# Norms from the solved blocks, block copies on three engines, and separate PSUM tiles in the opening of a DeltaNet and maxout kernel

## The chip, the cores and the metric

The kernel runs on one NeuronCore of a Trainium2 chip. Five engines work side by side, each through its own list of instructions in order: TensorE (PE in the profile, with PEld for its weight loads), VectorE (DVE), ScalarE (ACT), GpSimd (POOL) and SyncE (SP, which here only issues DMAs). They meet at semaphores. The metric is the device time of one execution in microseconds (us); four runs of the kernel before gave 524.16, 525.88, 523.24 and 526.01 us, a median of 525.02 us.

## The reference

Two stages follow one another. The first is a delta-rule recurrence over 768 steps, for 4 batches and 8 heads of width 48; the second is a feed-forward layer with three hidden projections whose maximum is taken:

```python
k_n = k / (np.linalg.norm(k, axis=-1, keepdims=True) + 1e-06)
for t in range(S):
    y[:, :, t] = np.einsum('bhd,bhde->bhe', q[:, :, t], state)
    v_old = np.einsum('bhde,bhd->bhe', state, kt)
    state = state + bt[:, :, :, None] * np.einsum('bhd,bhe->bhde', kt, vt - v_old)
x = y.transpose(0, 2, 1, 3).reshape(B * S, H * D)        # 3072 x 384
h = np.maximum(np.maximum(x @ w1, x @ w2), x @ w3)       # 3072 x 768
out = h @ w_out
```

## The kernel before, in words

The 768 steps are cut into 12 chunks of 64 steps, and two chunks make a group (six groups). Inside a chunk the recurrence becomes matrix work: `gram` (L434 to L460) forms the products of keys with keys (`at`) and of keys with queries (`pt`); a triangular system of the keys' products, scaled with beta, is solved; its solution `ut` is applied to the values (`new`, tile `p_u`), and the result `u` gives the outputs (`to_y`, `p_y`) and updates the state (`step`, `p_s`). The feed-forward layer of group m, `ffn(m)`, then works on the 512 tokens of its two chunks (`p_h`, `p_o`).

The kernel uses k without its norm: the rows of the solved system are scaled by the norm's square, and the values of a chunk are multiplied with the norms (`scale`, L286, on GpSimd). For groups 1 to 5 the norms are read off the diagonal of the keys' products inside `solve` (`norms_of`, L273). Group 0 does this differently: ScalarE squares the four first key tiles (`first_squares`, L312), VectorE sums them (L318), TensorE swaps the halves of the odd ones (`flipped`, L327), ScalarE copies the swapped sums (L1024) and `first_norms` takes root and a Newton step (L261 to L266).

The order on every engine is the order in which the program is written (`manual_schedule`), so the opening, L1006 to L1084, is an order by hand. Its steps, as the profile names them:

- Keys of the first two chunks are loaded (`kpad`), turned on TensorE (`turn`, `p_t`, copied out at L367), and multiplied (`keys`, `p_g`, copied out as `at` at L455).
- `to_blocks` (L497, L499) copies the 32 x 32 blocks on the diagonal into one tile, one copy for each of four partition blocks of a unit n, 16 copies in all. `first_blocks` (L503) transposes that tile on VectorE.
- `solve(0)` takes the norms from the diagonal (L539 on), scales, and eliminates in 15 steps of two VectorE instructions (L565, L569) inside 16 x 16 blocks. The result is transposed back (L573) and copied into `ut` for chunk 0, and later for chunk 1 (L584 on ScalarE, L586 on VectorE for chunk 0 and on GpSimd for chunk 1).
- The links of chunk 0 join the blocks: `halves_z` (`p_e`), `halves_u` (`p_f`), `join_z` (`p_z`), `join_u` (`p_j`). Then come `new` (`p_u`), `to_y` (`p_y`) and `to_x` (`p_x`, copied out as `xt` at L876 and L877), and with `xt` the first `p_h` of `ffn(0)`. For chunk 0 each link works on heads 0 to 3 and 4 to 7 in turn, each half in a PSUM tile of its own (`heads_of`); inside a half the two partition halves (`bb` 0 and 1) are copied out by ScalarE and VectorE, both from that one tile. PSUM tiles of this kind (`ps_two`) rotate through three buffers.
- Chunk 1's first link (`halves_z(1)`, again `p_e`) stands on TensorE between `to_y(0)` and `to_x(0)`. It reads `ut` of chunk 1.
- On GpSimd the order is: scale the values of chunk 0, scale the values of chunk 1 (loaded by `load_v(1)`, L139), two copies of `ut` for chunk 1 (L586), and then the sums that finish the converted weights (`w_sb`, L254).
- The weights arrive as 32-bit pieces that ScalarE takes apart in three instructions (`weights`, L238 to L240); VectorE shifts one part (L250) and GpSimd joins them. `some(conv, 1)` runs one such piece.

During `ffn(0)` the system of group 1 is solved on VectorE, with steps of 31 columns, between the steps of the feed-forward layer; from there on TensorE carries the kernel.

Of the kernel before, what the change touches and what calls it, by code (L numbers as in the profile page):

```python
# [9 lines left out]
FP32 = mybir.dt.float32  # L10
# [13 lines left out]
def kernel(  # L24
# [273 lines left out]
    nrm_0 = const.tile([128, 2, 2, H], FP32, name="nrm_0")  # L298

    ksum_0, kflip_0 = small("ksum0", 2, 2, H), small("kflip0", 2, H)  # L300

    def first_squares(units=range(4)):
        ksum, kflip, squares = ksum_0, kflip_0, []
        for n in units:
            c, g = divmod(n, 2)
            if n < 2:
                ksq = work.tile([128, H, D], FP32, name="ksq", tag="o_sb")
            else:
                ksq = in_wo(1).rearrange("p s r -> p (s r)")[
                    :, (n - 2) * H * D : (n - 1) * H * D  # L310
                ].rearrange("p (h d) -> p h d", h=H)
            nc.scalar.square(ksq, kpad[n][:, :, 0:D])  # L312
            squares.append(ksq)
        yield
        for n in units:
            c, g = divmod(n, 2)
            ksq = squares[n]
            nc.vector.tensor_reduce(  # L318
                out=kflip[:, c] if g else ksum[:, c, 0], in_=ksq,
                axis=mybir.AxisListType.X, op=ALU.add,  # L320
            )

    def flipped(kflip):
        p_n = ps_ffn([128, TOK], "p_n")[:, 0 : 2 * H]
        for bb in range(2):
            half = rows(1 - bb)
            nc.tensor.matmul(  # L327
                p_n[rows(bb)], ident[half, half],
                kflip[half].rearrange("p c h -> p (c h)"),
            )  # L330
        return p_n

    def first_norms():
        norm(nrm_0, ksum_0, small("root0", 2, 2, H), small("newton0", 2, 2, H))

# [185 lines left out]
    def solve(m):  # L521
# [15 lines left out]
        if m:  # L537
            norms_of(m, bl)
        nc.vector.reciprocal(bl, bl)  # L539
        nc.vector.tensor_tensor(out=bl, in0=bl, in1=bl, op=ALU.mult)  # L540
# [30 lines left out]
        if m == 0:  # L571
            back = in_rows(xs[0])
            nc.vector.transpose(out=back, in_=y.rearrange("p c i -> p i c"))  # L573
            yield
            for cc in range(2):
                for i in range(4):
                    bb, half = divmod(i, 2)
                    r = block(bb, half)
                    to = ut[cc][r, :, :, BL * half : BL * (half + 1)].rearrange(
                        "p g h i -> p (g h) i"  # L580
                    )
                    of = back[r, :, 16 * cc : 16 * (cc + 1)].rearrange("p i x -> p x i")
                    if half:
                        nc.scalar.copy(to, of)  # L584
                    else:
                        (nc.gpsimd if cc else nc.vector).tensor_copy(to, of)  # L586
                yield
            return
# [61 lines left out]
    def heads_of(c, name, w):  # L650
# [4 lines left out]
        for i, copy in enumerate(copies):  # L655
# [4 lines left out]
            )  # L660

    def span(hs):
        return slice(hs[0], hs[-1] + 1)
# [14 lines left out]

    def negated(bb, to, of, c=0):
        if bb and c < 1:  # L680
            nc.vector.tensor_scalar_mul(to, of, -1.0)
        else:
            nc.scalar.mul(to, of, -1.0)

    def halves_u(c):
        t, z = fine.pop(c), zs[c % NU]
        for hs, p_v, _ in heads_of(c, "p_f", BL):
            for i, h in enumerate(hs):
                for bb, g in TILES:
                    r = rows(bb ^ g)  # L690
                    nc.tensor.matmul(p_v[rows(bb), g, i], t[g][r, h], z[r, g, h])
            for f in (0, 1):
                for bb in range(2):
                    r = block(bb, f, HB)
                    negated(
                        bb,
                        ut[c % NU][r, :, span(hs), BL * f + HB : BL * (f + 1)],
                        p_v[r, :, :, HB * f : HB * (f + 1)],
                        c,
                    )  # L700

    def join_z(c):
        at = [ats.pop(2 * c + g) for g in range(2)]
        z, second = zs[c % NU], ut[c % NU][:, :, :, BL:C]
        for hs, p_v, _ in heads_of(c, "p_z", BL):
            for i, h in enumerate(hs):
                for bb, g in TILES:
# [3 lines left out]
                    )  # L711
            nc.scalar.copy(z[block(0), :, span(hs)], p_v[block(0)])
            copy = nc.vector.tensor_copy if c < 1 else nc.scalar.copy
            copy(z[block(1), :, span(hs)], p_v[block(1)])

    def join_u(c):
        z, t = zs[c % NU], t1[c % NU]
        u12 = ut[c % NU][:, :, :, BL:C]
        for hs, p_v, _ in heads_of(c, "p_j", BL):
            for i, h in enumerate(hs):  # L720
                for bb, g in TILES:
                    r = block(bb ^ g)
                    nc.tensor.matmul(p_v[block(bb), g, i], t[r, g, h], z[r, g, h])  # L723
            for bb in range(2):
                negated(bb, u12[block(bb), :, span(hs)], p_v[block(bb)], c)

# [89 lines left out]
    def to_x(c):  # L816
        m, cc = divmod(c, 2)
        if m not in xts:
            xts[m] = work.tile([128, KT, TOK], FP32, name="xt")
        y_f = yts.pop(c).rearrange("p g h d -> p g (h d)")  # L820
        p_x = ps_two("p_x")
        for g in range(2):
            for t in range(KT):
                nc.tensor.transpose(
                    p_x[:, g, t * 128 : (t + 1) * 128],
                    y_f[:, g, t::KT],
                    ident,
                )
        xt = xts[m][:, :, cc * 256 : (cc + 1) * 256].rearrange(
            "p t (g x) -> p g t x", g=2  # L830
        )
        copied(c, xt, p_x[:, :, 0 : KT * 128].rearrange("p g (t x) -> p g t x", t=KT))

# [26 lines left out]
    def turn_y(c):  # L860
# [8 lines left out]
        )  # L869

    def copied(c, to, of):

        if c:
            nc.scalar.copy(to, of)
        else:
            nc.scalar.copy(to[:, 0], of[:, 0])  # L876
            nc.vector.tensor_copy(to[:, 1], of[:, 1])  # L877


# [126 lines left out]
    turn(1, (0,), nc.vector.tensor_copy)  # L1006
    sums_0 = first_squares()
    some(sums_0, 1)
    keys(0, None, nc.vector.tensor_copy)
    some(sums_0, 1)  # L1010
    keys(1, None)
    to_blocks(0, (nc.gpsimd,) * 4)
    turn(2, (0,))
    turn(3, (0,))
    to_blocks(1, (nc.gpsimd,) * 4)
    keys(2, None, nc.vector.tensor_copy)
    keys(3, None, nc.vector.tensor_copy)
    to_blocks(2, (nc.scalar, nc.gpsimd, nc.scalar, nc.gpsimd))
    to_blocks(3, (nc.vector, nc.scalar, nc.vector, nc.scalar))
    first_blocks()  # L1020
    load_q(2, (nc.gpsimd, nc.gpsimd))
    some(solving, 1)
    p_n = flipped(kflip_0)
    nc.scalar.copy(ksum_0[:, :, 1], p_n.rearrange("p (c h) -> p c h", c=2))  # L1024
    turn(4, (0,))
    turn(5, (0,))
    keys(4)
    keys(5)
# [16 lines left out]
    gram(2, (1,), None, later=True)  # L1045
    turn(3, (1,))
    some(solving, HB + 1)
    halves_t(0)
# [3 lines left out]
    for c in range(2):  # L1052
        scale(c, nrm_0[:, c])
    some(conv, 1)
    halves_u(0)
# [176 lines left out]
```

## Time and profile before

| what | value |
|---|---|
| median of four runs | 525.02 us |
| profiled execution: time | 523.99 us |
| profiled execution: span | 522.3 us |
| TensorE busy | 495.5 us, 95% of the span |
| VectorE busy | 311.6 us, 60% |
| ScalarE busy | 164.2 us, 31% |
| GpSimd busy | 190.5 us, 36% |
| first `p_h` of `ffn(0)` starts | 51.63 us into the span |

The span is what lies between the first and the last recorded instruction of the profiled execution; its time is 1.7 us longer. A timeline line reads: start, duration, engine, line of the kernel, operation, tile written and tile read, shapes, count, and in brackets the idle time before with what ended it. A line of the stretches reads: stretch, its length, then for each engine its busy time and (in brackets) its instructions, then the granted TensorE clock (1.00 is full speed), the busy share of the DMA engines and GB/s.

### The profile page before, as it was taken

To read this page: it belongs to the slowest core of one execution; us is meant where nothing else is said; L and a number is where in the kernel's file an instruction comes from. 1 tells how busy PE (TensorE), PEld (TensorE's weight loads), DVE (VectorE), ACT (ScalarE), POOL (GpSimd) and SP (SyncE) were. 2 spreads that over 40 slices of the span, in tenths; PEclk is the share of its full clock that TensorE was granted. 3 is DMA by queue.
4 is the path that set the end of the run, shared out by engine and by line. 5 is a ranking of instruction groups with operands and counts; after the bars stand their busy time and mean duration, and the time that the engine had idled before them with its cause. 6 is when DMAs were issued, how large, how long until landed. Compare 5 with 4: busy or idle time off the path is not lost.

```text
span 522.3 us, 18030 instructions
## 1 busy us (share of the span) xinstructions
PE 495.5 (95%) x7840; PEld 306.9 (59%) x7840; DVE 311.6 (60%) x695; ACT 164.2 (31%) x302; POOL 190.5 (36%) x314
## 2 busy tenths in 40 slices
PE   7667998989999999999999999999999999999996
PEld 6556777855566655665555565655655555654453
DVE  6875999997996451699652988645896221111100
ACT  5557473777413142210153201252101411011000
POOL 7514255584474753951395770503130000000000
PEclk9865699999999999999999999999999999999999
DMA  8973968466026953454585453833333202220011
GB/s 110 208 164 106 162 161 145 128 147 200 15 72 151 177 102 67 128 133 116 110 155 127 116 133 92 166 48 92 82 105 86 43 3 63 62 60 0 0 30 32
DMA packets 108671, 53.47 MB, mean 102 GB/s; under 512 B 91760, under 2 KB 102928, under 8 KB 108592
## 3 DMA queue, kind: packets, MB, share of 16 engines
q1 hardware_dynamic: 97840, 34.44, 32.0%
q0 software_dynamic: 8640, 17.49, 13.5%
q8 instruction: 62, 1.02, 0.8%
q10 hardware_dynamic: 2112, 0.39, 0.5%
q14 instruction: 17, 0.14, 0.1%
HBM read 39.17 MB, written 13.11 MB: 100 GB/s over the span
## 4 chain that ended last, share of the span: by engine, by line
PE 77%; DVE 13%; ACT 3%; DMA 2%; issue 2%; SPq 1%; POOL 1%; DVEq 0%; ACTq 0%; POOLq 0%
PE p_h L926 33%; PE p_o L958 26%; DVE tmp L565 3%; PE p_g L438 3%; PE p_u L768 3%; DVE wo_sb L569 3%; PE p_m L906 2%; PE p_y L810 2%; DMA kmore<-in_k_dram 2%; PE p_k L740 2%; PE p_j L723 2%; PE p_s L791 1%; PE p_q L740 1%; SPq L120 1%; PE p_z L709 1%
## 5 line engine op out<-in xcount | busy, mean ns | idle before, releaser
L926 PE MATMUL p_h<-xt,w_sb 128*128 128x512 f32 (+1 forms) x522 | 219.0, 564 | 2.7 <-DVE h L940 1.3
L926 PEld LDWEIGHTS p_h<-xt,w_sb 128*128 128x128 f32 x522 | 96.1, 193 | 88.1 <-issue 79.9
L958 PE MATMUL p_o<-wo_sb,h 128*128 128x384 f32 x288 | 97.8, 489 | 0.0
L940 DVE TENSOR_TENSOR h<-h,p_h 128x512 f32<-128x512 f32 (+1 forms) x48 | 29.6, 617 | 89.7 <-PE p_h L926 89.5
L958 PEld LDWEIGHTS p_o<-wo_sb,h 128*128 128x128 f32 x288 | 53.7, 190 | 35.7 <-issue 0.5
L565 DVE TENSOR_TENSOR tmp<-x_bl,y_bl 128x31 f32<-128x31 f32 (+20 forms) x139 | 51.7, 372 | 4.1
L964 ACT COPY o_sb<-p_o 128x384 f32<-128x384 f32 x24 | 11.5, 479 | 132.9 <-PE p_o L958 126.8
L569 DVE TENSOR_TENSOR y_bl<-y_bl,tmp 128x31 f32<-128x31 f32 (+20 forms) x139 | 48.5, 349 | 4.8
L936 ACT ACTIVATE h<-p_h 128x512 f32<-128x512 f32 x30 | 17.9, 597 | 87.9 <-PE p_h L926 84.9
L958 PE MATMUL p_o<-w_sb,xt 128*128 128x384 f32 x120 | 42.0, 486 | 0.0
L396 POOL DMA_DIRECT2D turned<-in_q_dram x72 | 39.1, 551 | 3.5 <-POOL turned L391 3.0
L438 PE MATMUL p_g<-kqt 48*64 48x64 f32 (+1 forms) x1216 | 27.1, 236 | 6.4 <-DVE nt_bl L263 3.8
L438 PEld LDWEIGHTS p_g<-kqt 48*64 48x64 f32 x1216 | 24.0, 137 | 14.4 <-ACT kqt L367 7.4
L958 PEld LDWEIGHTS p_o<-w_sb,xt 128*128 128x128 f32 x120 | 22.8, 190 | 15.9
L287 POOL TENSOR_TENSOR v_t<-v_t,nrm 128x768 f32<-128x768 f32 x12 | 18.2, 1518 | 25.5 <-DVE nrm L266 12.4
L254 POOL TENSOR_TENSOR w_sb<-mant,up 128x384 int32<-128x384 int32 x18 | 18.3, 1018 | 24.8 <-DVE mant L250 19.1
L120 POOL DMA_DIRECT2D kpad<-in_k_dram x32 | 21.8, 689 | 14.6 <-PE p_s L791 13.2
L798 DVE TENSOR_TENSOR st<-st,p_s 48x768 f32<-48x768 f32 (+1 forms) x18 | 17.1, 949 | 15.0 <-PE p_s L791 14.8
L422 DVE TENSOR_TENSOR pt<-p_g,mask 128x512 f32<-128x512 f32 x20 | 13.7, 688 | 15.8 <-PE p_g L438 15.8
L139 POOL DMA_DIRECT2D v_t<-in_v_dram x12 | 9.9, 828 | 35.2 <-PE p_u L768 35.2
L391 POOL MEMSET turned<- 128x96 f32 x18 | 3.3, 191 | 44.0 <-DVE kqt L412 44.0
L768 PEld LDWEIGHTS p_u<-v_t,ut 64*64 64x64 f32 x768 | 13.5, 141 | 8.6 <-issue 7.4
(153 smaller groups left out, 628.1 us busy)
## 6 DMA issues: line engine op xcount, KB each, us to landing
w_bits<-in_moe_w_dram SPq DMA_DIRECT2D x14, 384.0 KB
out_dram<-o_sb SPq DMA_DIRECT2D x48, 96.0 KB
turned<-in_q_dram POOLq DMA_DIRECT2D x72, 48.0 KB, 2.5
kpad<-in_k_dram POOLq DMA_DIRECT2D x32, 96.0 KB, 5.4
y_x<-y SPq DMA_DIRECT2D x16, 192.0 KB
qall<-y_x SPq DMA_DIRECT2D x32, 96.0 KB
ut<-y_d SPq DMA_DIRECT2D x40, 64.0 KB
v_t<-in_v_dram SPq DMA_DIRECT2D x12, 192.0 KB
```

Source lines behind the costliest of these rows:

```text
L120: queues[bb].dma_start(out=dst[rows(bb ^ g), :, 0:D], in_=src[2 * bb + g, :, c * C : (c + 1) * C, :].rearrange("h p d -> p h d"),)
L254: nc.gpsimd.tensor_tensor(out=dst.bitcast(I32), in0=mant_v.bitcast(I32), in1=up_v, op=ALU.add)
L287: nc.gpsimd.tensor_tensor(out=vts[c], in0=vts[c], in1=nrm[:, :, :, None].to_broadcast([128, 2, H, D]), op=ALU.mult,)
L396: (queue, nc.gpsimd)[i].dma_start(out=t[p0 : p0 + 32, bb, at : at + NP * 2 * D].rearrange("p (j x) -> p j x", j=NP), in_=(k, q)[i][2 * bb ...
L438: nc.tensor.matmul(p_g[rows(bb ^ (g * i)), par, c0 : c0 + C * (1 + whole)], kq[:, 0], kq if whole else kq[:, i],)
L565: nc.vector.tensor_tensor(out=t_v, in0=row.to_broadcast(t_v.shape), in1=column.to_broadcast(t_v.shape), op=ALU.mult,)
L569: nc.vector.tensor_tensor(out=rest, in0=rest, in1=t_v, op=ALU.subtract)
L768: nc.tensor.matmul(p_v[rows(bb ^ g), g, i], ut[c % NU][rows(bb), g, h], rhs[rows(bb), g, h],)
L926: nc.tensor.matmul(p_h, w_sb[i][:, t, f * 128 : (f + 1) * 128], xt[:, t, lo : lo + w], start=(t == 0), stop=(t == KT - 1),)
L936: nc.scalar.activation(out=h, in_=p_h, func=mybir.ActivationFunctionType.Relu)
L940: nc.vector.tensor_tensor(out=h, in0=h, in1=p_h, op=ALU.max)
L958: nc.tensor.matmul(p_o, stays, moves, start=(n == 0), stop=(n == len(terms) - 1))
```

## The change

Five things are changed, all in the opening:

1. Norms of group 0. The squares, their sums, the swap on TensorE, the copy of the swapped sums, and the root with its Newton step are gone. `solve(0)` keeps its norms `bl` (the reciprocal goes to a tile of its own), and `first_norms` is one 128 x 32 transpose on VectorE.
2. Block copies. The 16 copies of `to_blocks` stood on GpSimd (10), ScalarE (4) and VectorE (2); now they stand on GpSimd (7), ScalarE (4) and VectorE (5). The first keys are turned and multiplied in another order and with other engines for the copies out.
3. Fourth block of chunk 0's `ut`: of the four copies of solved blocks VectorE takes three and ScalarE one (two and two before).
4. Evictions of `p_f` and `p_j` for chunk 0: the first four heads go to ScalarE alone; for the last four, each partition half has a PSUM tile of its own, one for ScalarE and one for VectorE. `p_z` of chunk 0 is copied out by ScalarE alone. `p_x` of chunk 0 stands in two tiles, one for each engine.
5. Order: `turn(4)` and `turn(5)` stand ahead of the first step of `solving`, and the first piece of weights is taken apart ahead of the elimination steps and not after the norms.

The core of the diff:

```diff
-    def first_squares(units=range(4)):
...
-            nc.scalar.square(ksq, kpad[n][:, :, 0:D])
...
-            nc.vector.tensor_reduce(
...
-    def flipped(kflip):
...
     def first_norms():
-        norm(nrm_0, ksum_0, small("root0", 2, 2, H), small("newton0", 2, 2, H))
+        nc.vector.transpose(out=nrm_0.rearrange("p c g h -> p (c g h)"), in_=bl_0[0])
...
         if m:
             norms_of(m, bl)
-        nc.vector.reciprocal(bl, bl)
+            nc.vector.reciprocal(bl, bl)
+        else:
+            bl_0.append(bl)
+            bl = small("inv_bl", BL)
+            nc.vector.reciprocal(bl, bl_0[0])
...
-                    if half:
+                    if i == 1 or cc and half:
                         nc.scalar.copy(to, of)
                     else:
                         (nc.gpsimd if cc else nc.vector).tensor_copy(to, of)
...
+    def negated_of(c, name, w):
+        if c:
+            p_v = ps_two(name)[:, :, 0 : H * w].rearrange("p g (h x) -> p g h x", x=w)
+            yield range(H), (p_v, p_v), (nc.scalar.mul,) * 2
+            return
+        p = [
+            ps_two(name)[:, :, 0 : NP * w].rearrange("p g (h x) -> p g h x", x=w)
+            for _ in range(3)
+        ]
+        yield range(NP), (p[0], p[0]), (nc.scalar.mul,) * 2
+        yield range(NP, H), (p[1], p[2]), (nc.scalar.mul, nc.vector.tensor_scalar_mul)
...
-            nc.scalar.copy(z[block(0), :, span(hs)], p_v[block(0)])
-            copy = nc.vector.tensor_copy if c < 1 else nc.scalar.copy
-            copy(z[block(1), :, span(hs)], p_v[block(1)])
+            for bb in range(2):
+                nc.scalar.copy(z[block(bb), :, span(hs)], p_v[block(bb)])
...
         p_x = ps_two("p_x")
         for g in range(2):
+            if g and not c:
+                p_x = ps_two("p_x")
...
+            if not c:
+                (nc.vector.tensor_copy if g else nc.scalar.copy)(xt[:, g], of[:, g])
+        if c:
+            nc.scalar.copy(xt, of)
...
-    sums_0 = first_squares()
-    some(sums_0, 1)
-    keys(0, None, nc.vector.tensor_copy)
-    some(sums_0, 1)
-    keys(1, None)
-    to_blocks(0, (nc.gpsimd,) * 4)
+    A, V, P = nc.scalar, nc.vector, nc.gpsimd
+    keys(0, None)
+    to_blocks(0, (P, P, P, P))
     turn(2, (0,))
+    keys(1, None, nc.vector.tensor_copy)
+    to_blocks(1, (V, P, V, P))
     turn(3, (0,))
-    to_blocks(1, (nc.gpsimd,) * 4)
-    keys(2, None, nc.vector.tensor_copy)
+    keys(2, None)
+    to_blocks(2, (A, P, A, A))
     keys(3, None, nc.vector.tensor_copy)
-    to_blocks(2, (nc.scalar, nc.gpsimd, nc.scalar, nc.gpsimd))
-    to_blocks(3, (nc.vector, nc.scalar, nc.vector, nc.scalar))
+    to_blocks(3, (V, A, V, V))
     first_blocks()
     load_q(2, (nc.gpsimd, nc.gpsimd))
-    some(solving, 1)
-    p_n = flipped(kflip_0)
-    nc.scalar.copy(ksum_0[:, :, 1], p_n.rearrange("p (c h) -> p c h", c=2))
     turn(4, (0,))
     turn(5, (0,))
+    some(solving, 1)
...
     turn(3, (1,))
+    some(conv, 1)
     some(solving, HB + 1)
...
-    some(conv, 1)
     halves_u(0)
```

## The prediction

> **What bounds the kernel now.** I read the stretches first, to see which engine carries which part of the span.
>
> ```profile
> 0.00:52.00 52.00, 34.75 (x903) 30.10 (x904) 36.02 (x86) 31.05 (x62) 23.90 (x48) 0.76 0.78 147
> 52.00:80.00 28.00, 26.44 (x638) 21.34 (x637) 26.74 (x63) 17.44 (x36) 11.75 (x13) 0.84 0.78 159
> 80.00:118.00 38.00, 34.48 (x689) 26.21 (x689) 35.71 (x72) 22.93 (x44) 24.57 (x33) 1.00 0.67 143
> 118.00:500.00 382.00, 381.90 (x5561) 218.95 (x5558) 213.11 (x477) 90.84 (x159) 130.28 (x223) 1.00 0.40 92
> ```
>
> TensorE (second column) is full from 118 us on. Of its 26.8 us without work, 17.25 lie in the first 52 us; from 52 to 118 VectorE is busy 62.45 of 66 us and the chain of waits runs through it almost alone. So a gain in the opening reaches the end by bringing the first `p_h`, and with it VectorE's dense stretch, forward.
>
> Next, the timelines of the opening, engine by engine. ScalarE and VectorE at the links of chunk 0:
>
> ```profile
> 34.80 0.54 ACT L238 ACTIVATE mant<-w_bits 128x384 f32<-128x384 f32 x1
> 36.21 0.24 ACT L683 ACTIVATE ut<-p_f 16x128 f32<-16x128 f32 x1
> 38.05 0.30 DVE L681 TENSOR_SCALAR ut<-p_f 16x128 f32<-16x128 f32 x1 [0.33 <-ACT ut L683]
> 39.77 0.76 DVE L714 COPY z<-p_z 32x256 f32<-32x256 f32 x2
> 41.35 0.85 DVE L681 TENSOR_SCALAR ut<-p_j 32x256 f32<-32x256 f32 x2
> 42.23 1.59 DVE L422 TENSOR_TENSOR pt<-pt,mask 128x512 f32<-128x512 f32 x1
> 50.93 0.56 DVE L877 COPY xt<-p_x 128x384 f32<-128x384 f32 x1 [3.30 <-ACT xt L876]
> ```
>
> The evictions of `p_f` start late (ScalarE takes weights apart until 36.33) and then take turns, each waiting for the other engine. Then GpSimd, and the queue that feeds it:
>
> ```profile
> 36.25 1.47 POOL L287 TENSOR_TENSOR v_t<-v_t,nrm 128x768 f32<-128x768 f32 x1 [12.41 <-DVE nrm L266]
> 41.80 1.47 POOL L287 TENSOR_TENSOR v_t<-v_t,nrm 128x768 f32<-128x768 f32 x1 [4.08 <-DMA v_t<-in_v_dram]
> 43.22 2.67 POOL L586 COPY ut<-x_bl 32x512 f32<-32x512 f32 x2
> ...
> 21.00 10.85 SPq L468 DMA_DIRECT2D at_d<-at  x16
> 34.50 1.34 SPq L139 DMA_DIRECT2D v_t<-in_v_dram  x2
> ```
>
> GpSimd's second scaling waits 4.08 us for the values of chunk 1, and the copies of chunk 1's `ut` are queued behind it until 45.89. Last, TensorE:
>
> ```profile
> 43.45 1.52 PE L768 MATMUL p_u<-v_t,ut 64*64 64x48 f32 x45 [0.95 <-issue]
> 44.70 2.04 PE L810 MATMUL p_y<-u,pt 64*64 64x48 f32 x64
> 46.52 2.38 PE L674 MATMUL p_e<-ut,at 64*64 64x32 f32 x64
> 48.84 1.55 PE L824 MATMUL p_x<-ident,y 128*128 128x128 f32 x6
> 51.63 2.90 PE L926 MATMUL p_h<-xt,w_sb 128*128 128x256 f32 x6 [1.25 <-DVE xt L877]
> ```
>
> The `p_e` at 46.52 is chunk 1's; it reads what GpSimd finished at 45.89, 0.6 us earlier: nearly a tie.
>
> **The change, part by part.** Times are of the profiled execution.
>
> *Head, to the transpose of the blocks at 13.03.* VectorE loses four sums (1.92 us, 8.23 to 10.15) and gains three copies (3 x 0.466 = 1.40); ScalarE loses four squares (2.5 us, with a wait of 0.61 for keys); GpSimd loses three of ten copies (1.29). Replayed in the new order with the rows' durations: the first product is copied out by ScalarE at 7.6 to 8.2, GpSimd's first four copies follow to 9.95 and its other three to 11.2; the last product is full at 10.7, VectorE copies it out (0.65) to 11.4, and then come VectorE's three copies to 12.5 or 12.9 and, after three for the product before, ScalarE's last to 12.3. So the transpose starts 0.1 to 0.5 us earlier, 0.3 taken. Worse is possible: were VectorE's five copies and GpSimd's seven to shut each other out, 5 x 0.466 + 7 x 0.431 = 5.35 us from 8.2 would give 13.55, 0.5 later. The rows speak against it: GpSimd's ten copies took 387 to 398 ns each, those beside VectorE's two (429 and 502 ns) too.
> [...]
>
> *`turn(4)`, `turn(5)` ahead of the solve.* Two ScalarE copies (1.08 us) go before the root; the root waits for the transpose (1.92 us) anyway, which covers them. TensorE's idle 12.07 to 15.84 shrinks; VectorE's solve (15.28 to 29.03) doesn't wait for that work.
>
> *Norms.* Five VectorE instructions (1.09 us), a root (0.23) and four matmuls (0.24) go; one transpose comes, 0.21 us by the nearest row (64 x 32, L281), at most 0.45 by the 128 x 256 one at L632. The first scaling on GpSimd ends near 35.2 and not 37.72; its reader `p_u` comes later than both: nothing by itself.
>
> *Blocks of `ut`.* Three VectorE copies (3 x 0.60) after 29.03 end at 30.84; ScalarE's two ended at 31.15: 0.3 earlier. The piece of weights moved ahead of them (1.53 us) fits into ScalarE's idle 1.24 us ahead of 29.03, and as only one ScalarE copy is left, a spill of 0.3 costs nothing. Without that cover: 0.3.
>
> *Evictions.* `p_f` is full at 35.7, its first half at 34.7. ScalarE is free at 34.65: four of 0.28 end at 35.9, two more at 36.5, VectorE's two beside them; before: 38.35. `p_z` runs 35.95 to 37.15, ScalarE empties it with four copies of 0.36 by 38.1 (before 40.53), VectorE's transposes (1.35) end at 37.85. `p_j` runs 37.9 to 38.95 (before to 41.31) and is emptied by 39.7 (before 42.20). So `p_u` starts near 39.4, 2 us earlier. I keep its stall of 0.95 or a little more, since the cause is no semaphore that this change touches: `p_u` ends at 42.4 to 43.0, `p_y` at 44.1 to 44.7, against 46.74: 2.0 to 2.6 us gained up to here.
>
> *What is late next.* Chunk 1's `p_e` can't follow at 44.4: GpSimd's copies wait behind the scaling at 41.80, that for a load, and the load for SyncE's queue, which issues without a pause from 0.81 to 33.11 in an order that the change leaves alone. What moves is only that VectorE's second mask (1.59 us where its siblings took 0.69, beside GpSimd's scaling and first copy) now comes near 40: the first copy took 1.52 us, the second 1.09; with 1.09 for both they end at 45.4, with 1.52 at 45.9. I take 45.5, near the undisturbed one. TensorE stands still about 1 us; `p_e` takes 2.16 (46.74 to 48.90) and ends at 47.6, `p_x` 1.49, at 49.15. The two `p_x` tiles let ScalarE copy while TensorE fills the second, so only VectorE's 0.56 follows and not 0.48 + 0.56: `xt` at 49.8, `p_h` at 50.0 (with 45.9: 50.35; before 51.63). Gain 1.3 to 1.8, taken 1.6.
>
> *From there on* nothing is edited. VectorE waits 4.3 us in all from 50 to 120, of which 3.3 is the `xt` wait above; so the stretch moves as a whole. The cover that could fail is TensorE at half clock (below).
>
> **Sum.** 523.99 - 1.6 = 522.4 for the profiled execution. It lies 1.0 below the median of the runs, so 525.0 - 1.6 = 523.4 us. The other parts lie beside that wait and drop out of the sum.
>
> **The clock.** From 32 to 60 us the granted clock is 0.50:
>
> ```profile
> 44.00:46.00 2.00, 2.00 (x82) 2.00 (x76) 0.98 (x2) 1.81 (x4) 1.83 (x2) 0.50 0.03 8
> 46.00:48.00 2.00, 1.92 (x71) 1.79 (x67) 0.94 (x3) 1.24 (x4) 1.22 (x2) 0.50 0.11 26
> 48.00:50.00 2.00, 2.00 (x39) 1.91 (x35) 0.00 (x0) 1.46 (x3) 0.78 (x1) 0.50 0.55 179
> ```
>
> Busy 5.92 of 6 us from 44 to 50, TensorE stays at half; it comes back near 61, with `p_h` running. I expect the same, shifted.
> [...]
>
> **Rivals.**
> *No gate at GpSimd* (0.10): the load lands earlier, `p_e` follows `p_y` at 44.4. Then `p_h` starts at 48.9, 2.7 earlier: 522.3. Against it stands the unbroken queue.
> *The clock comes back earlier* (0.15): one step of 3.4 us, as the cold stretch of 16.8 to 20.2 had, less at half speed is worth up to 1.7: 521.7. For it: TensorE is busy 2.00 of 2.00 from 52 to 60, so it matters there. Runs of one kernel spread over 2.8 us, which such steps would explain.
> *Nothing carries* (0.13): the evictions still take turns, or a later wait takes the gain: 525.0. Against: in the order built from the changed kernel VectorE's two evictions of `p_f` wait for TensorE and no longer for ScalarE.
> *Slower: the clock comes back later* (0.12), since the first `p_h` now falls elsewhere in the clock's steps. Each us more at half costs up to 0.5: from 3.2 us more it eats the gain (525.0), from 8.4 us more the kernel is slower by 2.6.
>
> **How the numbers follow.** The main case has 0.50, its own range 522.6 to 524.4 (gains of 1.3 to 1.8, and 0.7 for a median of few runs). The whole range reaches to the earlier clock less 0.5 and to the gain lost plus 0.6: 521.2 to 525.6. 0.5% is 2.6 us, about what a measurement of this kernel tells from no change; the bound is 522.4. Below it: 0.13 of the earlier clock, 0.06 of the missing gate, 0.11 of the main case's tail, 0.30. Over 527.6: 0.06 of the later clock. Within: 0.64.
>
> **What would show it.** In the profile after: VectorE's `p_f` evictions without a wait for ScalarE; GpSimd's second scaling still near 41.8 behind the load; chunk 1's `p_e` starting at 45.4 to 46.0 with TensorE idle before it; first `p_h` at 50.0 to 50.4. I am wrong if that `p_e` starts with `p_y`'s end, if the load lands at another time, or if the half clock ends more than 3 us from 60.

## The result, and the profile after

| | before | after |
|---|---|---|
| median of the runs | 524.92 us (78 runs) | 524.76 us (54 runs) |
| ratio after / before, 95% interval | | 0.9996 [0.9986, 1.0006] |
| profiled execution: time, span | 523.99, 522.3 us | 526.13, 524.4 us |
| first `p_h` of `ffn(0)` starts | 51.63 us | 53.85 us |

The change makes no difference that can be measured. The forecast's outcome (within 0.5%) and range hold; its gain of 1.6 us is not there: 0.2 us by the ratio, between 0.7 gained and 0.3 lost. The profiled execution of before lies 0.9 us below its median, that of after 1.4 us above, so the two pages differ by more than the kernels do, and I read several executions of the new order below.

The stretches of after (length, then busy time and instructions of TensorE, its weight loads, VectorE, ScalarE and GpSimd, then clock, DMA share, GB/s):

```profile
0.00:52.00 52.00, 36.68 (x894) 31.15 (x895) 30.60 (x73) 28.45 (x57) 22.18 (x44) 0.74 0.75 136
52.00:80.00 28.00, 24.97 (x563) 20.04 (x562) 25.63 (x62) 17.81 (x37) 10.01 (x11) 0.76 0.66 148
80.00:118.00 38.00, 37.09 (x707) 28.81 (x705) 35.55 (x72) 22.55 (x43) 24.35 (x31) 1.00 0.71 148
118.00:500.00 382.00, 381.14 (x5616) 218.60 (x5616) 214.91 (x480) 92.74 (x163) 132.32 (x226) 1.00 0.40 94
```

From 118 us on nothing differs but the shift. Between 52 and 80 us the mean clock is 0.76 where it was 0.84. ScalarE and VectorE in the timeline of after, around the solved blocks and the links:

```profile
28.73 0.58 ACT L335 COPY kqt<-p_t 128x512 f32<-128x512 f32 x1 [0.80 <-PE p_t L329]
29.21 0.55 ACT L238 ACTIVATE mant<-w_bits 128x384 f32<-128x384 f32 x1
31.32 1.05 ACT L556 COPY ut<-x_bl 32x512 f32<-32x512 f32 x1 [0.55 <-DVE x_bl L545]
36.87 1.69 ACT L673 ACTIVATE ut<-p_f 16x128 f32<-16x128 f32 x6 [0.24 <-PE p_f L669]
37.80 0.62 DVE L673 TENSOR_SCALAR ut<-p_f 16x128 f32<-16x128 f32 x2 [1.83 <-PE p_f L669]
42.35 1.52 ACT L690 COPY z<-p_z 32x256 f32<-32x256 f32 x4 [3.78 <-PE p_z L686]
```

The evictions do what the diff says: ScalarE takes six copies of `p_f` in 1.69 us, VectorE two beside them, and VectorE waits for TensorE and not for ScalarE. But the block begins late, and `p_z` comes 3.78 us after ScalarE is ready for it. TensorE and GpSimd in the same timeline:

```profile
11.36 1.99 PE L406 MATMUL p_g<-kqt 48*64 48x64 f32 x64
32.42 0.43 PE L658 MATMUL p_e<-ut,at 64*64 64x32 f32 x4 [3.72 <-ACT ut L556]
41.91 0.78 PE L686 MATMUL p_z<-ut,at 32*32 32x32 f32 x39 [3.30 <-issue]
46.27 1.41 PE L744 MATMUL p_u<-v_t,ut 64*64 64x48 f32 x41 [0.63 <-issue]
49.51 2.12 PE L658 MATMUL p_e<-ut,at 64*64 64x32 f32 x64
53.85 2.90 PE L899 MATMUL p_h<-xt,w_sb 128*128 128x256 f32 x6 [0.74 <-DVE xt L812]
...
42.21 1.47 POOL L287 TENSOR_TENSOR v_t<-v_t,nrm 128x768 f32<-128x768 f32 x1 [4.68 <-DMA v_t<-in_v_dram]
43.62 2.15 POOL L558 COPY ut<-x_bl 32x512 f32<-32x512 f32 x2
```

Three things to see. The 64 key products took 1.99 us where before has 1.18 (its line stands below). The record of the clock begins, at full speed, at 14.46 us here and at 6.54 in before; by these durations (also 1.13 us where before has 0.69 for the first 32) it was half until then (the mean clocks of the stretches count that time as full), so `first_blocks` began at 15.23 and not 13.03. Then `p_z` stops in its middle for 3.30 us without any semaphore. And GpSimd's second scaling waits for its load until 42.21, as before; it holds nothing here, since chunk 1's `p_e` comes only at 49.51.

`after_again` is the changed kernel once more: 524.19 us median, ratio 0.9993 [0.9968, 1.0018]. The execution in its profile took 528.24 us, the second longest of its twelve. In the opening it is nearer to the usual one, with the clock at full speed from 6.89 us on and `first_blocks` at 12.77:

> The changed kernel once more, for a second profiled execution. In the first one the blocks' transpose began at 15.23 us (13.03 before), with TensorE at half clock until 14.5 us (until 6.5 us before), and TensorE stood still 3.30 us inside p_z with no semaphore to wait for. Theory A (the stall inside p_z is an instruction fetch that got caught behind the loads of 33 to 41 us because this execution ran late): in an execution whose half clock ends early the transpose starts near 13 us, the stall is under 1.5 us and the first p_h starts at 50 to 51 us. Theory B (the new order of the first keys is slow by itself): the transpose starts at 14.5 us or later whatever the clock, and p_h no earlier than 52 us. Ratio to before in both: 0.998 to 1.001.

```profile
15.99 0.63 PE L329 MATMUL p_t<-ident,qall 128*128 128x128 f32 x4 [1.10 <-DMA qall<-in_q_dram]
28.66 0.58 ACT L335 COPY kqt<-p_t 128x512 f32<-128x512 f32 x1 [0.43 <-PE p_t L329]
30.72 1.04 ACT L556 COPY ut<-x_bl 32x512 f32<-32x512 f32 x1
31.80 0.71 DVE L618 STREAM_TRANSPOSE t<-ut 128x512 f32<-128x512 f32 x1 [1.08 <-ACT ut L556]
43.15 1.40 PE L744 MATMUL p_u<-v_t,ut 64*64 64x48 f32 x41 [2.17 <-issue]
46.69 1.92 PE L658 MATMUL p_e<-ut,at 64*64 64x32 f32 x60 [0.20 <-POOL ut L558]
50.83 2.90 PE L899 MATMUL p_h<-xt,w_sb 128*128 128x256 f32 x6 [0.74 <-DVE xt L812]
```

The same places in before:

```profile
9.80 1.18 PE L438 MATMUL p_g<-kqt 48*64 48x64 f32 x64 [0.37 <-ACT kqt L367]
27.20 0.58 ACT L367 COPY kqt<-p_t 128x512 f32<-128x512 f32 x1
31.18 0.71 DVE L646 STREAM_TRANSPOSE t<-ut 128x512 f32<-128x512 f32 x1 [0.94 <-ACT ut L584]
41.42 1.08 PE L768 MATMUL p_u<-v_t,ut 64*64 64x48 f32 x19
```

In `after_again` the blocks begin 0.3 us early, yet the first transposes of `ut` (31.80) come 0.6 us later than in before (31.18): they wait for ScalarE's copy, which stands behind the piece of weights, and that behind the last `kqt`. Then `p_u` stalls for 2.17 us, and GpSimd's `ut` holds chunk 1's `p_e`, as forecast, but for 0.20 us and not for about 1. The first `p_h` is 0.8 us earlier than in before; 1.6 was forecast.

### The profile page after: what moved, and what is told of

The parts are those of the page before. It is cut to its first block, busy times and chain, and to the rows that moved or that the text cites. A ratio compares the mean times of both kernels' runs of the same rounds, so it can differ in the third digit from the quotient of the medians.

```text
span 524.4 us, 18008 instructions
## 1 busy us (share of the span) xinstructions
PE 500.0 (95%) x7836; PEld 310.2 (59%) x7836; DVE 306.7 (58%) x685; ACT 163.5 (31%) x301; POOL 188.9 (36%) x311
## 4 chain that ended last, share of the span: by engine, by line
PE 78%; DVE 14%; ACT 3%; issue 2%; POOL 1%; DMA 1%; SPq 0%; DVEq 0%; ACTq 0%; POOLq 0%
PE p_h L899 33%; PE p_o L931 25%; PE p_g L406 4%; DVE tmp L537 3%; DVE wo_sb L541 2%; PE p_m L879 2%; PE p_y L786 2%; PE p_u L744 2%; PE p_k L716 2%; PE p_s L767 1%; PE p_q L716 1%; PE p_j L699 1%; PE p_z L686 1%; DVE mant L250 1%; DMA kpad<-in_k_dram 1%
## 5 line engine op out<-in xcount | busy, mean ns | idle before, releaser
L364 POOL DMA_DIRECT2D turned<-in_q_dram x72 | 39.1, 551 | 3.5 <-POOL turned L359 3.3
L406 PEld LDWEIGHTS p_g<-kqt 48*64 48x64 f32 x1216 | 25.9, 147 | 11.5 <-issue 7.1
L406 PE MATMUL p_g<-kqt 48*64 48x64 f32 (+1 forms) x1216 | 29.3, 248 | 2.8 <-ACT kqt L335 2.7
```

What stands on the lines that cost most here:

```text
L364: (queue, nc.gpsimd)[i].dma_start(out=t[p0 : p0 + 32, bb, at : at + NP * 2 * D].rearrange("p (j x) -> p j x", j=NP), in_=(k, q)[i][2 * bb ...
L406: nc.tensor.matmul(p_g[rows(bb ^ (g * i)), par, c0 : c0 + C * (1 + whole)], kq[:, 0], kq if whole else kq[:, i],)
```

## The experiments

**Which half of the change gains?** `head_only` has the new norms, block copies and order of keys and turns, with the old links. `links_only` has the old head with the new `ut` copies, evictions, `p_x` and place of the first piece of weights.

```diff
 head_only, against after:
-        for hs, p_v, negate in negated_of(c, "p_f", BL):
+        for hs, p_v, _ in heads_of(c, "p_f", BL):
...
 links_only, against after:
+    some(solving, 1)
+    p_n = flipped(kflip_0)
...
     turn(4, (0,))
     turn(5, (0,))
-    some(solving, 1)
```

> Norms from the diagonal, block copies on three engines, new order of the first keys and turns; the links of chunk 0 (copies of ut, evictions of p_f, p_z, p_j, p_x, place of the first weights' piece) stay as before. Theory B (the head costs what the links gain): slower than before by 1 to 2 us, ratio 1.002 to 1.004, transpose of the blocks 1 to 2 us later than 13.03. Theory A (the head is neutral, the links' gain is lost at TensorE's instruction fetch): ratio 0.999 to 1.001.

> The links of chunk 0 as changed (copies of ut, separate PSUM tiles, p_z on ScalarE, p_x in two tiles, first weights' piece earlier); norms by squares and sums, block copies and key order as before. Theory B: the links' gain shows, ratio 0.996 to 0.9975 (1.3 to 2 us), first p_h at 49.9 to 50.4 us against 51.63. Theory A: TensorE's stall without a semaphore moves forward and grows by what the evictions save, ratio 0.999 to 1.001.

Measured: `links_only` 523.87 us, ratio 0.9972 [0.9948, 0.9996], so 1.5 us faster (0.2 to 2.7). `head_only` 526.28 us, ratio 1.0018 [0.9998, 1.0039], 0.9 us slower (0.1 faster to 2.0 slower). The product, 0.9990, is what both together gave, within the intervals. So the links by themselves bring about the 1.6 us that I forecast. By the medians the head, which I had at 0.3 gained and then hidden, takes most of it back; that is less firm, since its interval includes no change, and the interval of `links_only` overlaps that of after. The links in `links_only`, where `p_z` stalls for 0.61 us besides:

```profile
31.18 0.71 DVE L646 STREAM_TRANSPOSE t<-ut 128x512 f32<-128x512 f32 x1
40.05 0.84 PE L772 MATMUL p_u<-v_t,ut 64*64 64x48 f32 x19 [0.18 <-issue]
42.19 1.53 PE L772 MATMUL p_u<-v_t,ut 64*64 64x48 f32 x45 [1.30 <-issue]
49.90 2.90 PE L927 MATMUL p_h<-xt,w_sb 128*128 128x256 f32 x6 [0.74 <-DVE xt L840]
```

How the head can cost time, in one execution of `head_only`:

```profile
16.67 1.08 PE L329 MATMUL p_t<-ident,qall 128*128 128x128 f32 x4 [1.97 <-DMA qall<-in_q_dram]
29.37 0.58 ACT L335 COPY kqt<-p_t 128x512 f32<-128x512 f32 x1 [0.43 <-PE p_t L329]
29.98 2.12 ACT L556 COPY ut<-x_bl 32x512 f32<-32x512 f32 x2
32.13 0.71 DVE L618 STREAM_TRANSPOSE t<-ut 128x512 f32<-128x512 f32 x1 [2.24 <-ACT ut L556]
```

Blocks begin at 12.59 and VectorE has solved them at 28.65, 0.4 us earlier than in before. But TensorE, at its turns sooner, runs out of loaded queries and waits 1.97 us; its clock falls to half at 16.52 us and stays there (0.50 from 20 to 60 us), `turn` and `gram` run at half speed (four products of `p_t` in 1.08 us, in `after_again` in 0.63), ScalarE copies the last `kqt` at 29.37 (before: 27.20), and only then comes to `ut`. The transposes wait 2.24 us for that copy, 0.94 in before.

**GpSimd's order.** `pool_first`: chunk 1's `ut` copies on GpSimd go ahead of its second scaling and no longer wait for a load that they don't need.

```diff
-            for cc in range(2):
-                for i in range(4):
+            for cc, order in ((0, (0, 1, 2, 3)), (1, (0, 2)), (1, (1, 3))):
+                for i in order:
...
-    for c in range(2):
-        scale(c, nrm_0[:, c])
+    scale(0, nrm_0[:, 0])
+    some(solving, 1)
+    scale(1, nrm_0[:, 1])
```

> The changed kernel with GpSimd's two copies of chunk 1's ut ahead of its scaling of chunk 1's values, so that they no longer wait for that load. If GpSimd's order holds the gain back (the step of the prediction), the ratio to before is 0.996 to 0.9975, about 1 to 1.5 us under the changed kernel. If TensorE's own stalls or the head hold it back, it equals the changed kernel within 0.001.

Measured: 522.78 us, ratio 0.9964 [0.9946, 0.9981]; 1.7 us below after, and the interval does not touch that of after.

```profile
36.41 2.14 POOL L558 COPY ut<-x_bl 32x512 f32<-32x512 f32 x2
41.77 1.61 POOL L287 TENSOR_TENSOR v_t<-v_t,nrm 128x768 f32<-128x768 f32 x1 [3.22 <-DMA v_t<-in_v_dram]
45.80 1.90 PE L658 MATMUL p_e<-ut,at 64*64 64x32 f32 x64
49.92 2.90 PE L899 MATMUL p_h<-xt,w_sb 128*128 128x256 f32 x6 [0.74 <-DVE xt L812]
```

Chunk 1's `p_e` follows `p_y` without a gap and without a releaser, with the same load still landing late. This is the gate that the prediction named; it put its absence at 1.1 us (522.3 against 523.4). The medians show that GpSimd's order costs time. That all of the 1.7 us is this one wait isn't shown: `p_e` waited for GpSimd for 0.20 us in `after_again`, not at all in the first profile of after, and for 1.47 and 0.70 us in `piece_between` below.

**The head's two suspects.** `turns_back` puts `turn(4)` and `turn(5)` behind the first step of `solving` again. `piece_between` lets the first piece of weights follow ScalarE's `ut` and `p_e` copies. `all_three` has both and GpSimd's order.

```diff
 turns_back:
+    some(solving, 1)
     turn(4, (0,))
     turn(5, (0,))
-    some(solving, 1)
 piece_between:
-    some(conv, 1)
     some(solving, HB + 1)
     halves_t(0)
     halves_z(0)
+    some(conv, 1)
     gram(3, (1,), None, later=True)
```

> The changed kernel with turn(4) and turn(5) behind the first step of the solve again, as before the change. Theory C (in the new order TensorE reaches the products of keys 4 to 7 early, then stands waiting for the loads of q and keys, its clock drops to half at 16 to 20 us and stays there, so that its turns and products end at 28.6 to 29.3 us and not at 27.2, and ScalarE's copy of ut starts at 30.7 to 31.1 and not at 28.9): full clock from about 20 to 30 us, TensorE done at 27 to 28 us, ScalarE's copy of ut at 29.5 or earlier, 1 us gained, ratio to before 0.9965 to 0.9985. Theory D (the order of the turns is indifferent): as the changed kernel, 0.999 to 1.0005, ScalarE's copy at 30.5 or later.

> The changed kernel with the first piece of weights (1.8 us on ScalarE) taken apart between the evictions of p_e and of the product after it, no longer ahead of the copy of ut. Theory C with ScalarE as its last step: the copy of ut starts when ScalarE has copied the last turn, at about 29.3 us, VectorE's transposes of ut start behind its own third copy at 30.7 and not at 31.8 to 32.2, about 1 us gained, ratio 0.9965 to 0.9985. If it gains nothing, what delays p_e is not ScalarE's queue.

> The changed kernel with GpSimd's copies of chunk 1's ut ahead of its second scaling, turn(4) and turn(5) behind the first step of the solve, and the first piece of weights between the two evictions. If the three costs are separate and lie on the one path, first p_h at 48.5 to 49.5 us and ratio to before 0.993 to 0.9955. If TensorE's stalls without a semaphore take what is freed, 0.996 to 0.997, as with GpSimd's order alone.

Measured: `turns_back` 524.48 us, 0.9993 [0.9966, 1.0020]; `piece_between` 524.75 us, 0.9983 [0.9957, 1.0008]; `all_three` 523.14 us, 0.9968 [0.9938, 0.9998]. Neither suspect alone moves the time by what can be measured, and both together add nothing that can be measured to GpSimd's order. The timeline of `piece_between` shows the gain arise and go:

```profile
28.77 1.04 ACT L556 COPY ut<-x_bl 32x512 f32<-32x512 f32 x1 [0.15 <-DVE x_bl L545]
30.68 0.71 DVE L618 STREAM_TRANSPOSE t<-ut 128x512 f32<-128x512 f32 x1
42.05 1.40 PE L744 MATMUL p_u<-v_t,ut 64*64 64x48 f32 x41 [2.28 <-issue]
44.12 1.54 POOL L287 TENSOR_TENSOR v_t<-v_t,nrm 128x768 f32<-128x768 f32 x1 [9.13 <-DMA v_t<-in_v_dram]
46.68 0.43 PE L658 MATMUL p_e<-ut,at 64*64 64x32 f32 x4 [1.47 <-POOL ut L558]
47.80 1.92 PE L658 MATMUL p_e<-ut,at 64*64 64x32 f32 x60 [0.70 <-POOL ut L558]
51.94 2.90 PE L899 MATMUL p_h<-xt,w_sb 128*128 128x256 f32 x6 [0.74 <-DVE xt L812]
```

ScalarE copies `ut` as soon as it is there and the transposes no longer wait (30.68, 1.1 us earlier than in `after_again`): the place of the piece did cost that microsecond. Then TensorE stalls 2.28 us in `p_u`, the load for GpSimd lands later still, and `p_h` comes at 51.94, where before has it. In `turns_back` the last turn waited for its queries all the same (0.62 us, until 27.45), and the transposes began at 31.70. Why in detail the head costs 0.9 us by its median stays open: the unchanged kernel shows the same late `kqt` in one execution of two (below). One difference the profiles do show is where the clock's long stretch at half speed (13.65 us or more) begins: at 15.67 to 24.70 us in the five executions with the two turns ahead of the solve, at 24.34 to 30.44 in the seven with the turns behind it and no added products.

**The stall without a semaphore.** It stands in `p_z` or `p_u` in every execution with the new links: 3.30 + 0.63 us in after, 0.41 + 2.17 in `after_again`, 0.42 + 2.39 in `all_three`, 0.53 + 0.19 + 0.63 in `pool_first`. In the DMA view of after, the packets of kind "instruction" between 38.5 and 40.5 us (packets, MB, share), and over the whole execution:

```profile
q8 instruction: 1, 0.02, 4.6%
...
q8 instruction: 61, 1.00, 0.8%
```

Between 33.0 and 38.5 us there is none. 61 packets for the 15,672 instructions of TensorE and its weight loads make one for every 257. The packet that comes inside the stall lands at 40.2 us, and `p_z` goes on at 41.91; in `all_three` it lands at 41.1 and `p_u` goes on at 42.46, in `after_again` at 41.7 and 43.15. I read it as the next part of TensorE's program, late because the DMA engines are full of loads just then (99.4% of their time from 38.5 to 40.5 us goes to the packets of q1). The place fits. With the new head and nothing added, TensorE stops after 25 of the 64 products of `p_z` or after 23 of those of `p_u`; from one place to the other are 39 + 64 + 23 = 126 products, 252 instructions with their weight loads, about what one packet holds. In `all_three_warm` (below), where 20 products more stand ahead of the links, it stops 20 products sooner, after 5 and after 3. (The short stops ahead of the first product of `p_u`, 0.19 to 0.43 us, are not at such a place.) `pieces_later` is `all_three` with two transfers of weights moved from SyncE's queue, ahead of chunk 1's values, to GpSimd's, behind its second scaling:

```diff
-    for _ in range(2):
-        fetch(nc.sync)
     blocks(1)
     load_v(1)
...
     scale(1, nrm_0[:, 1])
+    for _ in range(2):
+        fetch(nc.gpsimd)
```

> The version with three edits, and the two weight transfers issued after 32 us moved from SyncE's queue, ahead of the keys and values of chunk 1, to GpSimd's queue behind its second scaling. Theory that TensorE's stall without a semaphore (2.39 us at p_u in the three-edit version) is its instruction refill standing behind those loads: the values of chunk 1 land near 38 and not 40.55, the stall shrinks to 0.9 or less, the first p_h comes at 48 and not 49.52, and the ratio is 0.9935 to 0.9965 unless a later half-speed stretch takes it back. Rival, the stall is the refill's own time whatever else moves: it stays near 2 us, p_h at 49 to 49.5, ratio 0.996 to 0.998.

Measured, in six runs: 521.58 us, ratio 0.9937 [0.9905, 0.9969], 3.3 us faster than before and faster than after, whose interval it does not touch; the interval of `all_three` it does overlap. In its timeline:

```profile
40.31 1.40 PE L744 MATMUL p_u<-v_t,ut 64*64 64x48 f32 x41 [0.91 <-issue]
45.94 0.55 ACT L238 ACTIVATE mant<-w_bits 128x384 f32<-128x384 f32 x1 [2.53 <-POOL w_sb L254]
48.38 2.90 PE L899 MATMUL p_h<-xt,w_sb 128*128 128x256 f32 x6 [2.37 <-ACT xt L812]
```

The packet lands 2.7 us earlier than in `all_three` (38.5), the stall is 0.41 + 0.91 us and not 0.42 + 2.39, and `p_h` comes 1.1 us earlier. The values of chunk 1 landed no sooner (GpSimd's scaling of them starts at 41.91 us, in `all_three` at 41.78): that part of the expectation fails. TensorE's instructions are the same in both kernels. In the three executions with the transfers moved the packet for `p_u` lands at 38.5 to 39.1 us, in the eleven others at 39.95 us or later, also in `piece_between` (40.3), where `p_u` starts at nearly the same time (38.89 and 38.52). So the stall goes with what else is being loaded; that the loads delay the packet is the reading that fits, not a thing that a row names.

`third_piece_later` then moved the third piece of weights behind the first `xt`, since ScalarE waits 2.53 us ahead of it for GpSimd.

```diff
     to_y(0)
-    some(conv, 1)
     fetch(nc.sync)
     halves_z(1)
     to_x(0)
     some(conv, 1)
+    some(conv, 1)
```

> The version with the two weight transfers moved, and one more edit: the third piece of weights is taken apart behind the first xt and not ahead of chunk 1's p_e copy. In the version without it ScalarE waited 2.53 us at that piece for GpSimd's w_sb, and the first p_h 2.37 us for ScalarE's xt. Theory that GpSimd's second scaling, behind its load, still holds the first p_h, now through ScalarE's queue: that wait leaves ScalarE's place ahead of xt, the first p_h starts at 46.4 to 47.0 and not 48.38; the end gains 0.3 to 1.5 us more, less than the 1.8 of p_h, because VectorE, which carries the stretch after 46 us, had its own xt already at 46.05; ratio 0.990 to 0.994. Rival, VectorE's stretch alone sets the end: p_h comes earlier and the ratio stays at 0.9937 within 0.001, or p_h is held by another wait and doesn't move.

Measured: 522.40 us, ratio 0.9956 [0.9933, 0.9979]. The wait is gone and the first `p_h` starts at 47.47, 0.9 us earlier, not 1.4 to 2.0, held by VectorE's `xt` at 46.77. No gain in the time follows; the rival expectation comes nearer.

**The clock.** `all_three_warm` adds to `all_three`, ahead of the links, ten products of 128 columns that nobody reads (20 instructions in the profile); `pieces_later_warm` adds two of 512 columns to `pieces_later`.

```diff
     turn(3, (1,))
+    busy(10, ident)
     some(solving, HB + 1)
```

> The kernel before in this list, and ten further products of the identity on TensorE, whose result nobody reads, in its idle time ahead of chunk 0's first link. If dense 128 x 128 work holds the clock where the links' small products don't, the links run at full clock for the first 5 to 10 us, and p_e to p_j are faster by up to 2 us: first p_h at 47 to 48.5, ratio 0.990 to 0.994. If the clock drops all the same or the added work delays p_e (ten take about 2.5 us at full clock, 4.9 at half), the ratio is that of the kernel without them or up to 0.004 more.

> The version before with two products of 512 columns, whose result nobody reads, on TensorE ahead of the links, where it waits for the solve. Theory that dense products before the links hold the granted clock: full clock through the links, to 35 us or more, p_e, p_f, p_z and p_j at about half their time, the first p_h at 46.5 to 47.5; and a half-speed stretch afterwards, in the first p_h, which gives back 1 to 3 us, so that the ratio is 0.994 to 0.999. Rival, two products are too short: half speed from about 28 us on as without them, p_h as without them within 0.5 us.

The stretches of 28 to 38 and 114 to 128 us, first in `all_three`, then in `all_three_warm`:

```profile
28.00:38.00 10.00, 7.90 (x258) 6.82 (x258) 7.69 (x15) 6.99 (x17) 3.49 (x3) 0.50 0.70 174
114.00:128.00 14.00, 13.18 (x304) 7.37 (x305) 10.12 (x26) 10.46 (x20) 6.74 (x9) 0.88 0.64 205
```

```profile
28.00:38.00 10.00, 6.99 (x272) 5.96 (x272) 8.47 (x15) 6.41 (x16) 3.50 (x3) 1.00 0.83 181
114.00:128.00 14.00, 11.78 (x236) 6.24 (x235) 8.43 (x23) 8.20 (x17) 4.73 (x6) 0.76 0.57 182
```

With ten dense products ahead the clock stays full to 38.04 us, through most of the links, and the first `p_h` starts at 47.71, 1.8 us earlier than in `all_three`. Yet the time is 525.20 us, 1.0014 [0.9985, 1.0044]. In this execution the clock falls later, from 119.95 to 126.78 us, and between 114 and 128 us TensorE gets through 236 products and not 304. That the added products bring this about isn't shown: six of the thirteen executions without the ten products have a step of 3.41 us at half speed between 114 and 123 us too, `all_three` among them, and seven have none. With two products the clock held to 32.71 us only and `p_h` came at 48.29, 0.1 earlier than without them: 522.11 us, 0.9933 [0.9901, 0.9964], the same as `pieces_later`.

**The kernel before, once more.**

> The kernel before, unchanged, profiled a second time. Its first profiled execution lay 1.0 us below its median, and TensorE's granted clock in it had no half-speed stretch after 61.16 us. Theory that the later half-speed stretches belong to chance (where TensorE's short idle times fall) and not to the changed kernel: this execution shows one, of 3.4 us or a multiple, between 57 and 127 us, or a profiled time near 524 without one. Rival, that they belong to the new order: none after 62 us, and the first p_h at 51.6 as before.

525.20 us, with the clock at half from 24.34 to 55.06 and from 61.89 to 65.30 us; `kqt` copied last at 29.43, the transposes at 32.20, the first `p_h` at 51.88, the end 1.1 us later than in the first profile. So a late `kqt` and a later stretch at half speed are no property of the new order. What they can cost shows in the stretch of 60 to 76 us, in the first profile of before and in `after_again`:

```profile
60.00:76.00 16.00, 15.00 (x438) 11.77 (x439) 15.25 (x38) 11.24 (x22) 7.72 (x9) 0.96 0.57 142
```

```profile
60.00:76.00 16.00, 12.75 (x258) 9.94 (x251) 13.28 (x33) 7.22 (x14) 7.71 (x9) 0.68 0.54 139
```

At a clock of 0.68 TensorE did 258 products where it did 438 (not all of one size), and VectorE, the bound there, was busy 13.28 us and not 15.25. Counting the same TensorE instructions from the end of its list, `after_again` is 0.8 us ahead of before's first profile at 54 us, 1.7 behind at 105, and 4.2 behind at the end, after another stretch at half speed from 119.53 to 122.94.

## Why the prediction was right, and where its size was wrong

- **Outcome and range: right.** 524.76 lies in 521.2 to 525.6 and within 0.5%, which had 0.64. The predicted 523.4 misses by 1.4 us, nearly the whole gain. That outcome and range hold is no support for the sum: both take in a gain of nothing. Two of the signs by which the prediction was to be known as wrong came: in the first profile of after chunk 1's `p_e` starts with the end of `p_y`, and in `after_again` the half clock ends at 54.68 us, 5 us before 60, and comes back from 64.92 to 75.16. A slip in the working: the main case's own range begins, by its numbers, at 522.5 and not at 522.6.
- ***Head*: right where the clock starts early.** Forecast 0.3 us earlier than 13.03; measured 12.39 to 13.04 in the ten executions with the new head besides the first of after, `after_again` (12.77) and `head_only` (12.59) among them. VectorE and GpSimd did not shut each other out to the 13.55 that was to give (15.23 in after is the late clock). But the prediction read too much out of the rows when it took the copies for undisturbed: in `after_again` VectorE's first block copy took 281 ns, the next, beside GpSimd's, 400, and GpSimd's beside them 544 where its others took 386 to 398. So the 429 and 502 ns of VectorE's two in before were no undisturbed length either; the price is by these rows some 0.1 to 0.2 us a copy.
- ***`turn(4)`, `turn(5)` ahead of the solve*: priced at nothing by looking at the wrong engine.** “VectorE's solve doesn't wait for that work” holds, but ScalarE's queue does: from `turn` over `kqt` to the copy of `ut`. TensorE came early to queries not yet loaded (1.10 us in `after_again`, 1.97 in `head_only`) and soon went on at half speed (from 20.54 and 16.52 us). The two executions differ from before by 0.6 and 1.0 us at the transposes; putting the turns back did not by itself bring a measurable gain.
- ***Blocks of `ut`*: wrong.** “A spill of 0.3 costs nothing” took ScalarE's idle 1.24 us as cover; the cover was gone, since `kqt` ended at 29.2 and not 27.8. ScalarE's `ut` began at 30.72 and not by 29.3; in `piece_between` the transposes start 1.1 us earlier. With the old head the cover held: in `links_only` the last `kqt` is copied by 28.20, and the transposes (31.18) wait for nothing. This step failed, together with the one above.
- ***Evictions*: right.** From the first transposes of `ut` to the first `p_u` both executions of before take 10.24 us (31.18 to 41.42, 32.20 to 42.44); `after_again` takes 8.29, `all_three` 8.22, `pool_first` 8.84, `links_only` 8.87: 1.4 to 2.0 gained where `p_z` does not stall for long, 2 forecast. `head_only`, with the old evictions, takes 10.12.
- **“I keep its stall of 0.95 or a little more”: too small.** 1.1 to 3.9 us in the executions with the new links, where, by the reading above, a packet falls among the loads; it is the second term that failed. Nor is it a fixed length: in six executions with the new links and the transfers in their old place (`after_again`, `links_only`, `pool_first`, `turns_back`, `piece_between`, `all_three`) `p_u` starts at 38.89 to 41.31 us and goes on after its stall at 42.05 to 43.15; before's first profile has 41.42 and 43.45. An earlier `p_u` thus mostly waits longer, and behind the stall 0.3 to 1.4 us are gained.
- ***What is late next*: the right gate, the size open.** Taking it out gains 1.7 us by the medians (`pool_first`), and 522.78 us is near the *No gate* rival's 522.3, but its first `p_h` was put at 48.9 and came at 49.92. Where it stands, TensorE waited 0.20 us in `after_again` and not about 1; in the first profile of after the gate is idle, since everything before it was late.
- ***From there on*, and *The clock*: partly wrong.** A shift at 54 us does reach the end in some executions (`links_only` −1.7 and −1.8 us, `pool_first` −1.7 at both), but in `after_again`, `head_only` and `all_three_warm` 2.7 to 8 us are lost between there and the end, and in `all_three`, `turns_back` and `third_piece_later` 2.1 to 3.2; stretches at half speed fall into that time (the clock was 0.68 from 60 to 76 us in `after_again`, 0.75 in `turns_back`, and 0.88 from 114 to 128 us in `head_only` and `all_three`). I had the clock only as one stretch that ends near 60. The wide spread of single runs (after: 521.29 to 528.41) fits this.
- **The rivals.** *Nothing carries* is the one whose time was met (525.0). Its first reason does not hold, as the evictions no longer take turns; its second, a later wait that takes the gain, does in part: TensorE's stall is one. The rest sits ahead of the links.

What stays open: how the head's 0.9 us (0.1 gained to 2.0 lost) divides between the late queries and the clock, and how much the new place of the piece of weights adds to it where both changes meet. Single executions show each of them; no run tells them apart by its median.

## What to carry to other kernels

A step that is moved on an in-order engine is costed by what stands behind it on that engine in the worst execution, not in the one profile at hand: an idle 1.24 us there was cover in one execution and gone in the next. When links of small products get faster, look next for what the other queues hold back without need: GpSimd's copies behind a load that they don't read were worth 1.7 us, and two loads that nobody needed yet, moved away, another 1.6 by the medians, with intervals that overlap. And an opening that is 1 to 3 us earlier must be measured over many runs: in `after_again` 5.0 us were lost between 54 us and the end, with stretches of 10.24 and 3.41 us at half speed in between.

## What the runs showed of the hardware

- TensorE's half-speed stretches came in whole steps of 3.41 us (before: 16.78 to 20.20; `all_three_warm`: 38.04 to 44.86, two steps). A nearly busy TensorE did not bring the full clock back with small products: in `after_again` it was busy 7.06 of the 8 us from 44 to 52 and the clock stayed at 0.50, while ten dense products of 2.40 us in all were followed by full clock until 38.04 us, 8 us beyond their end (in `all_three`, without them, it fell at 27.78).
- The longer stalls named “issue” in the links ended 1.1 to 1.9 us after a packet of kind “instruction” had landed (after: 40.2 and 41.91 us; `all_three`: 41.1 and 42.46). The packets have 16 KB each, one for some 257 instructions of TensorE and its weight loads. That such a stall is TensorE's own program arriving late is a reading that fits; no row names it. With 64 small products in a link, 128 instructions, these numbers put such a packet in about every second link.
- A clock held up early need not show at the end: `all_three_warm` was 5.3 us ahead of before's profile at 54 us and 2.6 us behind at the end, with 6.83 us at half speed in between; single executions don't show whether the one brought the other.
